# Three loads of an attention and mixer kernel made smaller: q of twelve pairs, v of all, four weight tiles

## The chip, the cores and the metric

The kernel runs on one core of a Trainium2 chip. The metric is the device time of one execution in microseconds (us). Five engines work side by side, each through its own queue in order: PE (TensorE, matmuls; PEld is its weight load), DVE (VectorE), ACT (ScalarE), POOL (GpSimd) and SP (SyncE), which here does nothing but issue transfers. The transfers themselves run on 16 DMA engines.

## The reference

Causal attention over 4 batches, 12 heads, 448 tokens and a head width of 64, and behind it two mixer blocks on the joined heads (448 tokens by 768 channels). Cut to what matters:

```python
scores = q @ k.T / 8, upper triangle masked
x = (softmax(scores) @ v), heads joined            # (4, 448, 768)

h  = relu(x.T @ w_tok1) @ w_tok2                    # tokens 448 -> 256 -> 448
u  = x + h.T
x2 = u + relu(u @ w_ch1) @ w_ch2                    # channels 768 -> 1536 -> 768

theta = x2 @ w_theta
y  = w_tok_r @ (x2 * cos(theta)) + w_tok_i @ (x2 * sin(theta))
u2 = x2 + y
out = u2 + relu(u2 @ w_ch)
```

All weights of the mixers arrive as float64 and are rounded on the chip; large products are made of fp16 pieces (high and low part, three matmuls for each product).

## The kernel before

**Pairs.** Heads are taken two at a time: 6 pairs for each of the 4 batches, 24 in all, numbered 0 to 23. Of each pair seven tiles of scores are made (`TILES`): one tile of the first 64 tokens of both heads, and for i = 1, 2, 3 one of 128 tokens for each head h. `scores` runs, for a tile, the matmuls of q and k (line 358, and 360 for the low part of k), DVE's mask and row minimum (367, tile `mx`) and ACT's exponential (369). Pairs 0 to 11 (`NATIVE`) use q and k as float32; pairs 12 to 23 are the **split pairs**, where q and k are turned into a rounded high part and a rest. For these q was put into the input twice, in partitions 0 to 63 and again in 64 to 127, and loaded whole (line 288): ACT writes the high part of all 128 partitions to `qs` (297), DVE the rest to partitions 64 to 127 (298).

**Values.** `v_raw` holds nine blocks of 64 columns for a pair. Blocks 0 to 5 are the tokens from 64 on of both heads, blocks 6 and 7 the first 64 tokens with one head each, block 8 the first 64 of both heads one above the other. Pairs 0 to 7 (`NATPV`) multiply with float32 values and transpose their attention on PE (376, copied by ACT in 378); `pv` does it on line 407. Pairs 8 to 23 split the attention into two fp16 parts (`ph`: ACT on 160, DVE on 388) and have a DMA transpose it into `pt` (line 391, on SP's queue), and multiply on lines 416 and 424. Their values are scaled and split too: `value_squares` (ACT, 124) and `value_split` (POOL writes `v_hi` on 163, DVE the rest over `v_raw` on 323).

**Units.** The channel products are 96 units, 24 for each batch, each of 18 fp16 matmuls of 448 columns (helper `mm3`, lines 231 to 233) with one weight tile `ws` of 384 KB. Each of the 24 weight tiles is first fetched raw (`raw`, 768 KB), rounded by ACT, POOL and DVE (177, 130, 185, 186), split into a `ws` tile (POOL 163, DVE 197) and stored to DRAM (`round_store`, line 581); each unit then loads its tile from there (`load_unit`, `stream_tile`, line 226). Unit n of batch 0 could load its tile only after it was stored. Tiles `ws` come from a ring of 8 buffers.

**Order.** The steps (7 tiles by 24 pairs) form one loop; `UNIT_STEPS` says at which step a unit is put in, `ROUNDINGS` at which step a weight tile is handled. Within that, a scheduler sets the order of instructions on each engine from priorities and its own estimate of durations, so an edit in one place can move work elsewhere. Names such as `w_c_1_4_115` in the orders below are weight tiles in DRAM: half 1, tile 4, and a running number (99 to 104 and 111 to 116 belong to units 12 to 23, numbers from 93 to units 24 on when they are loaded again).

Of the kernel before, what the change touches and what calls it, by code (L numbers as in the profile page):

```python
# [8 lines left out]
F32 = mybir.dt.float32  # L9
F32R = mybir.dt.float32r  # L10
F16 = mybir.dt.float16
# [7 lines left out]
P = 128  # L19
# [14 lines left out]
ROUND_BITS, ROUND_FETCH, ROUND_SPLIT, ROUND_STORE = 1, 2, 3, 5  # L34
LATE_CONVERT = 16
FIRST_UNIT, DENSE, RATE = 53, 88, (42, 29)
UNIT_STEPS = [FIRST_UNIT + n * (DENSE - FIRST_UNIT) // 14 if n < 14 else
# [17 lines left out]
def fused(ctx, tc, q, k, v, w_tok1, w_tok2, w_ch1, w_ch2, w_theta, w_tok, w_ch, out):  # L55
# [220 lines left out]
    def prep(b, pr):  # L276
        qr = ap2.tile([P, 2 * S], F32, tag="qk_raw", name="q_raw", bufs=2)
        if b * NPR + pr in NATIVE:
            kr = ap2.tile([P, 2 * S], F32, tag="kh", name="k_pad")
            for t, src in ((kr, k), (qr, q)):  # L280
                (nc.vector if b * NPR + pr == 0 else nc.gpsimd).memset(t[64:128], 0.0)
                if b * NPR + pr == 0 and t is qr:
                    for c in (slice(0, 2 * P), slice(2 * P, 2 * S)):
                        nc.scalar.dma_start(out=t[0:64, c], in_=src[b, pr, 0:64, c])
                else:
                    loads[b * NPR + pr] = nc.sync.dma_start(out=t[0:64], in_=src[b, pr, 0:64])
        else:
            loads[b * NPR + pr] = nc.sync.dma_start(out=qr, in_=q[b, pr])
            kr = ap2.tile([P, 2 * S], F32, tag="qk_raw", name="k_raw", bufs=2)
            nc.sync.dma_start(out=kr, in_=k[b, pr])  # L290
        vr = ap2.tile([P, 9 * D], F32, tag="v_raw", name="v_raw")
        nc.sync.dma_start(out=vr, in_=v[b, pr])
        if b * NPR + pr in NATIVE:
            qs, kh, kl = qr, kr, None
        else:
            qs = ap2.tile([P, 2 * S], F32R, tag="qs", name="qs")
            copy_to(pick("qhi"), qs, qr)
            rest_to(pick("qlo"), qs[64:128], qr[64:128], qs[64:128])
            kh = ap2.tile([P, 2 * S], F32R, tag="kh", name="kh")
# [14 lines left out]
    def value_split(n):  # L314
# [4 lines left out]
        power(None, scale, values.pop(n), unit)  # L319
        hi = ap2.tile([P, 9 * D], F16, tag="v_hi", name="v_hi", bufs=2)  # L320
        copy_to("P", hi, vr, scale)
# [71 lines left out]

    def twice(ap):
        return ap.unsqueeze(1).to_broadcast([P, 2, D])

    def pv(pp, i, h):
# [3 lines left out]
        if pp.native_pv:  # L401
            pt = pp.pts[i, h]
            blks = [8] if i == 0 else [6 + h] + [2 * u + h for u in range(i)]
            for u, vt in enumerate(blks):
                n = 2 * D if reg < 7 * D else D
                rhs = twice(pp.v[0][:, vt * D:(vt + 1) * D]) if i == 0 else pp.v[0][:, vt * D:vt * D + n]
                pp.pv = nc.tensor.matmul(pp.ps[:, reg:reg + n], lhsT=pt[:, u], rhs=rhs,  # L407
                                 start=(u == 0), stop=(u == len(blks) - 1))
            return
# [4 lines left out]
        if i == 0:  # L414
            for n, (blk, c) in enumerate(((0, 0), (0, 1), (1, 0))):
                pp.pv = nc.tensor.matmul(pp.ps[:, 0:2 * D], lhsT=pt[:, blk], rhs=twice(pp.v[c][:, 8 * D:9 * D]),
                                         start=n == 0, stop=n == 2)
            return
# [159 lines left out]
    def round_store(j):  # L578
        n = ROUNDINGS[j][1]
        if n >= 0:  # L580
            nc.sync.dma_start(out=jobs[n][1], in_=rounding.pop(j))
            stored.add(n)

    made = [0]
# [370 lines left out]
def _lay(inputs):  # L955
# [26 lines left out]
    zero = np.zeros_like(a0)  # L982
    for x, y in ((a0, np.where(native, a0, zero)), (np.where(native, b0, zero), b0), (a0, b0)):
        blocks.append(np.concatenate([x, y], axis=2))
# [41 lines left out]
```

## Time and profile before

| what | value |
|---|---|
| median of 3 runs | 872.34 us (870.30 to 873.48) |
| the profiled execution | 871.68 us |
| its span in the trace | 869.9 us |
| mean granted TensorE clock over the span | 0.998 |
| PE busy | 839.3 us (96%) |
| DVE, ACT, POOL busy | 598.9, 531.3, 265.6 us |
| moved by DMA | 151.99 MB, 175 GB/s on average |

The attention fills the first 500 us or so; units run beside it from about 110 us on, and the second mixer block follows. A matmul's busy time includes its way through the array, so a busy PE can still have small gaps that the rows don't show as idle.

### The profile page before, as it was taken

The numbers are of one execution on the slowest core, as the hardware profiler recorded it, in microseconds if no ns is written. First come the engines' busy times: TensorE is split into PE (matmuls) and PEld (weight loads), VectorE is DVE, ScalarE is ACT, GpSimd is POOL, SyncE is SP. The second block draws the span as 40 slices with busy tenths as digits, with TensorE's granted clock in tenths as the row PEclk, the third lists the DMA queues.
The fourth block names the chain that finished last, engine by engine and source line by source line (L and its number), as shares of the span: only waits on it lengthen the run. The fifth ranks groups of instructions, "written<-read, shape, count | busy, mean of one in ns | idle before, by whom it ended". The sixth has DMA issues, their size and how long they took to land.

```text
span 869.9 us, 16014 instructions
## 1 busy us (share of the span) xinstructions
PE 839.3 (96%) x5699; PEld 532.7 (61%) x5699; DVE 598.9 (69%) x1294; ACT 531.3 (61%) x1223; POOL 265.6 (31%) x445
## 2 busy tenths in 40 slices
PE   7999998899899999999999999999999999999997
PEld 6988856565657566576756655565555555555554
DVE  6788787999988556567774367669747548567541
ACT  6798786777767637367653276547647447456441
POOL 4366564547662220413222035331111001101000
PEclk9999999999999999999999999999999999999999
DMA  6866869999999976856475597702613123131012
GB/s 217 258 208 201 269 198 271 261 310 294 289 255 313 280 226 140 233 132 125 141 173 203 186 278 265 227 30 73 197 40 108 40 90 98 40 119 58 25 45 75
DMA packets 121024, 151.99 MB, mean 175 GB/s; under 512 B 76848, under 2 KB 88048, under 8 KB 120944
## 3 DMA queue, kind: packets, MB, share of 16 engines
q1 hardware_dynamic: 120400, 149.95, 59.4%
q0 software_dynamic: 384, 0.79, 0.4%
q8 instruction: 45, 0.74, 0.3%
q10 hardware_dynamic: 160, 0.23, 0.1%
q14 instruction: 35, 0.29, 0.1%
HBM read 110.56 MB, written 22.81 MB: 153 GB/s over the span
## 4 chain that ended last, share of the span: by engine, by line
PE 67%; DMA 10%; DVE 8%; ACT 5%; issue 5%; POOL 5%; SPq 0%; ACTq 0%; POOLq 0%; DVEq 0%
PE ps_mm L232 15%; PE ps_mm L231 15%; PE ps_mm L233 15%; DMA pt<-ph 5%; PE ps_sc L358 3%; PE ps_sc L231 3%; PE ps_sc L232 3%; PE ps_sc L233 3%; PE ps_pv L407 2%; DMA raw_w<-in_w_theta_dram 1%; PE ps_pv L424 1%; ACT junk L124 1%; ACT sb L369 1%; DVE sb L367 1%; PE ps_mm L376 1%
## 5 line engine op out<-in xcount | busy, mean ns | idle before, releaser
L231 PE MATMUL ps_mm<-h,ws 128*128 128x448 f16 x432 | 151.7, 354 | 1.6 <-DVE g L140 1.0
L232 PE MATMUL ps_mm<-h,ws 128*128 128x448 f16 x432 | 152.7, 354 | 0.1
L233 PE MATMUL ps_mm<-h,ws 128*128 128x448 f16 x432 | 152.5, 354 | 0.0
L231 PEld LDWEIGHTS <-ws 128*128 128x128 f16 x720 | 70.5, 98 | 67.2 <-issue 5.3
L233 PEld LDWEIGHTS <-ws 128*128 128x128 f16 x720 | 70.5, 98 | 63.9 <-issue 3.7
L232 PEld LDWEIGHTS <-ws 128*128 128x128 f16 x720 | 70.5, 98 | 62.5 <-issue 5.2
L369 ACT ACTIVATE sb<-sb,mx 128x320 f32<-128x320 f32 (+3 forms) x168 | 89.1, 533 | 25.6 <-DVE mx L367 25.0
L231 PE MATMUL ps_mm<-ut,ws 128*128 128x448 f16 x288 | 101.1, 353 | 1.4 <-DMA rawt<-x2d 1.3
L232 PE MATMUL ps_mm<-ut,ws 128*128 128x448 f16 x288 | 101.5, 353 | 0.8 <-DVE ut L197 0.8
L233 PE MATMUL ps_mm<-ut,ws 128*128 128x448 f16 x288 | 101.6, 353 | 0.0
L367 DVE CUSTOM_DVE_ANT_0 sb<-ps_sc,mask 128x320 f32<-128x320 f32 (+3 forms) x168 | 73.4, 455 | 17.7 <-PE ps_mm L376 11.3
L124 ACT ACTIVATE junk<-acc 128x448 bf16<-128x448 f32 x72 | 41.2, 572 | 59.1 <-DVE acc L912 41.3
L358 PE MATMUL ps_sc<-k_pad,q_raw 128*128 128x192 f32 (+3 forms) x168 | 56.9, 441 | 9.1 <-DMA k_pad<-in_k_dram 4.3
L787 POOL TENSOR_SCALAR tmp<-tmp 128x384 f32<-128x384 f32 x28 | 15.6, 556 | 148.6 <-ACT tmp L786 145.6
L388 DVE SCALAR_TENSOR_TENSOR ph<-sb,ph 128x128 f16<-128x128 f32 (+1 forms) x64 | 46.8, 736 | 19.0 <-ACT ph L160 18.3
L163 POOL TENSOR_SCALAR h<-t 128x448 f16<-128x448 f32 x48 | 35.2, 735 | 75.7 <-ACT t L497 75.2
L497 ACT ACTIVATE t<-ps_mm,c_scale 128x448 f32<-128x448 f32 x48 | 30.0, 625 | 41.3 <-PE ps_mm L233 36.2
L160 ACT ACTIVATE ph<-sb 128x128 f16<-128x128 f32 (+1 forms) x64 | 39.6, 625 | 25.6 <-DMA pt<-ph 25.3
L499 DVE TENSOR_TENSOR h<-t,h 128x448 f16<-128x448 f32 x48 | 32.0, 670 | 27.0 <-POOL h L163 26.9
L130 POOL TENSOR_SCALAR raw<-raw 128x768 f32<-128x768 f32 (+2 forms) x34 | 35.4, 1041 | 41.6 <-ACT wf L177 37.0
L231 PE MATMUL ps_sc<-th,ut 128*128 128x384 f16 x144 | 46.9, 326 | 0.0
L233 PE MATMUL ps_sc<-th,ut 128*128 128x384 f16 x144 | 46.8, 326 | 0.0
(218 smaller groups left out, 2119.4 us busy)
## 6 DMA issues: line engine op xcount, KB each, us to landing
ws<-w_c SPq DMA_DIRECT2D x120, 384.0 KB, 4.6
raw<-in_w_ch_dram SPq DMA_DIRECT2D x30, 768.0 KB, 5.6
w_c<-ws SPq DMA_DIRECT2D x30, 384.0 KB, 4.3
v_raw<-in_v_dram SPq DMA_DIRECT2D x24, 288.0 KB, 4.9
q_raw<-in_q_dram SPq DMA_DIRECT2D x12, 448.0 KB, 4.2
k_raw<-in_k_dram SPq DMA_DIRECT2D x12, 448.0 KB, 5.4
x2d<-acc SPq DMA_DIRECT2D x24, 224.0 KB, 3.8
acc<-x2d SPq DMA_DIRECT2D x24, 224.0 KB, 2.6
```

Source lines behind the costliest of these rows:

```text
L124: nc.scalar.activation(j[:, 0:src.shape[-1]], src, AF.Square, accum_out=dst)
L130: nc.gpsimd.tensor_scalar(out=dst, in0=a, scalar1=b, scalar2=c, op0=ALU.mult, op1=ALU.mult)
L160: nc.scalar.activation(dst, src, AF.Copy, scale=scale)
L163: e.tensor_scalar(out=dst, in0=src, scalar1=scale, scalar2=0.0, op0=ALU.mult, op1=ALU.add)
L231: nc.tensor.matmul(ps, lhsT=ka(a[:, 0]), rhs=kb(b[:, 0]), start=first, stop=False)
L232: nc.tensor.matmul(ps, lhsT=ka(a[:, 0]), rhs=kb(b[:, 1]), start=False, stop=False)
L233: return nc.tensor.matmul(ps, lhsT=ka(a[:, 1]), rhs=kb(b[:, 0]), start=False, stop=last)
L358: nc.tensor.matmul(ps[:, 0:n], lhsT=lhs, rhs=cut(pp.kh), start=True, stop=pp.kl is None)
L367: pp.first = nc.vector.tensor_tensor_reduce(out=sb, in0=src, in1=msk, op0=ALU.add, op1=ALU.min, scale=-0.125, scalar=3.0e38, accum_out=pp. ...
L369: pp.last = nc.scalar.activation(sb, sb, AF.Exp, bias=pp.mx[:, j:j + 1], scale=-1.0, accum_out=pp.sm[:, 2 + j:3 + j])
L388: nc.vector.scalar_tensor_tensor(out=lo, in0=both, scalar=PSC, in1=hi, op0=ALU.mult, op1=ALU.subtract)
L499: gates[0] = nc.vector.tensor_tensor(out=t[:, 1], in0=f, in1=t[:, 0], op=ALU.subtract)
```

## The change

Three things are done.

1. For the split pairs q is loaded into partitions 0 to 63 alone (224 KB in place of 448 KB). ACT makes the high part in partitions 0 to 63, and DVE writes the rest to partitions 64 to 127 from both inputs in partitions 0 to 63.
2. The block 8 of v goes away: the tile has 8 blocks (256 KB in place of 288 KB). The first 64 tokens use blocks 6 and 7 side by side. A float32 product of the second head (h = 1) then writes 64 columns where, for i = 1 and 2, it wrote 128. `v_hi` and the split have 512 columns in place of 576.
3. The weight tiles of units 20 to 23 stay in their `ws` buffer after the store and are used from there; their four loads of 384 KB go away.

```diff
+FIRST_DIRECT = 20
...
-            loads[b * NPR + pr] = nc.sync.dma_start(out=qr, in_=q[b, pr])
+            loads[b * NPR + pr] = nc.sync.dma_start(out=qr[0:64], in_=q[b, pr, 0:64])
...
-        vr = ap2.tile([P, 9 * D], F32, tag="v_raw", name="v_raw")
+        vr = ap2.tile([P, 8 * D], F32, tag="v_raw", name="v_raw")
...
-            copy_to(pick("qhi"), qs, qr)
-            rest_to(pick("qlo"), qs[64:128], qr[64:128], qs[64:128])
+            copy_to(pick("qhi"), qs[0:64], qr[0:64])
+            rest_to(pick("qlo"), qs[64:128], qr[0:64], qs[0:64])
...
-        hi = ap2.tile([P, 9 * D], F16, tag="v_hi", name="v_hi", bufs=2)
+        hi = ap2.tile([P, 8 * D], F16, tag="v_hi", name="v_hi", bufs=2)
...
-            blks = [8] if i == 0 else [6 + h] + [2 * u + h for u in range(i)]
+            blks = [6] if i == 0 else [6 + h] + [2 * u + h for u in range(i)]
             for u, vt in enumerate(blks):
-                n = 2 * D if reg < 7 * D else D
-                rhs = twice(pp.v[0][:, vt * D:(vt + 1) * D]) if i == 0 else pp.v[0][:, vt * D:vt * D + n]
+                n = 2 * D if h == 0 else D
...
-                pp.pv = nc.tensor.matmul(pp.ps[:, 0:2 * D], lhsT=pt[:, blk], rhs=twice(pp.v[c][:, 8 * D:9 * D]),
+                pp.pv = nc.tensor.matmul(pp.ps[:, 0:2 * D], lhsT=pt[:, blk], rhs=pp.v[c][:, 6 * D:8 * D],
...
-            nc.sync.dma_start(out=jobs[n][1], in_=rounding.pop(j))
+            w = rounding.pop(j)
+            nc.sync.dma_start(out=jobs[n][1], in_=w)
             stored.add(n)
+            if n >= FIRST_DIRECT:
+                loaded[n] = w
```

The scheduler's order changes with it. Line numbers of the changed kernel are one higher behind the new constant, and two or three lower behind `twice`, which is gone. On SP, where the last two weight tiles of batch 0 are stored, before:

```order
L581 DMA w_c_1_4_115<-ws 128x1536
L226 DMA ws<-w_c_1_4_115 128x1536
L391 DMA_TRANSPOSE pt<-ph 128x14x128
L391 DMA_TRANSPOSE pt<-ph 128x2x128
L173 DMA raw<-in_w_ch_dram 128x1536
L581 DMA w_c_1_5_116<-ws 128x1536
...
L226 DMA ws<-w_c_1_5_116 128x1536
L226 DMA ws<-w_c_0_0_93 128x1536
```

And in the changed kernel, from the same store on:

```order
L579 DMA w_c_1_4_115<-ws 128x1536
L293 DMA v_raw<-in_v_dram 128x512
L289 DMA q_raw<-in_q_dram 64x896
L291 DMA k_raw<-in_k_dram 128x896
L392 DMA_TRANSPOSE pt<-ph 128x6x128
L392 DMA_TRANSPOSE pt<-ph 128x10x128
L227 DMA ws<-w_c_0_0_93 128x1536
L227 DMA ws<-w_c_0_1_94 128x1536
L227 DMA ws<-w_c_0_2_95 128x1536
L579 DMA w_c_1_5_116<-ws 128x1536
```

The two loads that read back what was stored just ahead of them are gone, and the loads for units 24 to 26 (numbers 93 to 95) now stand ahead of the last store.

On PE, at the first scores of pair 12 (the `ps_sc` tiles; line 358 is the product with k's high part, 360 that with its low part; `ps_mm` with `wt2` is the token product, with `ident` a transpose), before:

```order
L358 MATMUL ps_sc_2696<-kh_2447,qs_2444 128x256
L360 MATMUL ps_sc_2696<-kl_2449,qs_2444 128x256
L358 MATMUL ps_sc_2742<-kh_2447,qs_2444 128x256
L360 MATMUL ps_sc_2742<-kl_2449,qs_2444 128x256
L358 MATMUL ps_sc_2776<-kh_2447,qs_2444 128x256
L360 MATMUL ps_sc_2776<-kl_2449,qs_2444 128x256
```

And in the changed kernel:

```order
L359 MATMUL ps_sc_2696<-kh_2447,qs_2444 128x256
L361 MATMUL ps_sc_2696<-kl_2449,qs_2444 128x256
L359 MATMUL ps_sc_2742<-kh_2447,qs_2444 128x256
L454 MATMUL ps_mm_2371<-ident2_128,x1_192 128x64
L234 MATMUL ps_mm_2361<-wt2_185,h1_2323 128x448
...
L361 MATMUL ps_sc_2742<-kl_2449,qs_2444 128x256
L232 LDWEIGHTS ws_2094
L232 MATMUL ps_mm_2388<-h2_1518,ws_2094 128x448
...
L359 MATMUL ps_sc_2776<-kh_2447,qs_2444 128x256
L361 MATMUL ps_sc_2776<-kl_2449,qs_2444 128x256
```

Three tiles of scores stood in a row; now the token products stand inside the second, and seven unit matmuls ahead of the third. Through pairs 12 to 18 the scores stand on average 18 unit matmuls further back than before, with most of the products `pv` of the same pairs near their old places; from pair 20 on the two orders agree within five.

## Rows read from the trace of the kernel before

**Rows 1.** The page: busy us (share of span) and instructions of each engine.
```profile
PE 839.3 (96%) x5699; PEld 532.7 (61%) x5699; DVE 598.9 (69%) x1294; ACT 531.3 (61%) x1223; POOL 265.6 (31%) x445
```
**Rows 2.** Busy time by stretch; the first line names the columns.
```profile
core 0: us, PE busy (x) PEld busy (x) DVE busy (x) ACT busy (x) POOL busy (x), PEclk, DMA share, GB/s
0.00:125.00 125.00, 115.97 (x793) 96.94 (x794) 99.19 (x263) 98.76 (x269) 69.36 (x111) 1.00 0.71 224
125.00:310.00 185.00, 170.96 (x1387) 113.00 (x1386) 160.20 (x360) 129.64 (x313) 91.53 (x130) 0.99 1.03 278
310.00:575.00 265.00, 263.51 (x1858) 161.38 (x1857) 162.55 (x344) 142.93 (x330) 76.95 (x142) 1.00 0.67 191
575.00:870.00 295.00, 288.81 (x1667) 161.35 (x1665) 176.98 (x329) 159.97 (x312) 27.75 (x64) 1.00 0.23 74
```
**Rows 3.** Chain of waits inside 125 to 310 us, share of it by line.
```profile
by line: DMA pt<-ph 23.6%; issue 17.4%; DMA k_raw<-in_k_dram 4.1%; DMA w_c<-ws 3.7%; DVE sb L367 3.7%; ACT sb L369 3.5%; ACT ph L160 2.9%; DVE ut L197 2.6%; DVE ph L388 2.5%; DVE wf L186 2.0%; POOL f L130 1.9%; POOL ws L163 1.8%; POOL sm L4
```
**Rows 4.** Waits of PE, 125 to 310 us: total us, times, longest.
```profile
PE ps_sc L358 <- DVE mx L367: 2.7, 4, 1.0
PE ps_pv L416 <- POOL v_hi L163: 2.1, 2, 1.6
...
PE ps_pv L424 <- DMA pt<-ph: 1.1, 2, 0.8
...
PE ps_mm L231 <- DMA ws<-w_c: 0.6, 1, 0.6
```
**Rows 5.** Waits of all engines, same stretch: ACT for the attention's transposes.
```profile
ACT ph L160 <- DMA pt<-ph: 18.6, 12, 3.4
```
**Rows 6.** DMA, same stretch: total; issues with count, KB each, us to landing.
```profile
DMA packets 52210, 51.36 MB, mean 278 GB/s; under 512 B 40336, under 2 KB 41104, under 8 KB 52188
...
ws<-w_c SPq DMA_DIRECT2D x31, 384.0 KB, 6.2
...
q_raw<-in_q_dram SPq DMA_DIRECT2D x9, 448.0 KB, 4.6
...
v_raw<-in_v_dram SPq DMA_DIRECT2D x8, 288.0 KB, 5.2
...
q_raw<-in_q_dram SPq DMA_DIRECT2D x2, 224.0 KB, 7.3
```
**Rows 7.** Timeline of SP's queue, then of PE: start us, us, instruction, idle before.
```profile
247.53 0.38 SPq L581 DMA_DIRECT2D w_c<-ws  x1
253.43 0.32 SPq L226 DMA_DIRECT2D ws<-w_c  x1
...
269.33 0.36 PE L231 MATMUL ps_mm<-h,ws 128*128 128x448 f16 x1 [0.57 <-DMA ws<-w_c]
```
**Rows 8.** Groups by form: tiles, shapes, count; busy us, mean ns; idle before.
```profile
L407 PE MATMUL ps_pv<-v_raw,pt 128*128 128x128 f32 x240 | 33.8, 278 | 0.9 <-ACT pt L378 0.8
...
L163 POOL TENSOR_SCALAR v_hi<-v_raw,sv 128x576 f16<-128x576 f32 x16 | 16.4, 1024 | 0.0
...
L323 DVE SCALAR_TENSOR_TENSOR v_raw<-v_raw,sv,v_hi 128x576 f16<-128x576 f32 x16 | 15.2, 952 | 5.2 <-POOL v_hi L163 5.2
...
L167 DVE TENSOR_TENSOR qs<-q_raw,qs 64x896 fp32r<-64x896 f32 x12 | 14.2, 1180 | 0.7 <-ACT qs L160 0.3
...
L407 PE MATMUL ps_pv<-v_raw,pt 128*128 128x64 f32 x64 | 8.1, 267 | 0.0
```
**Rows 9.** Busy time by stretch, columns as in rows 2.
```profile
125.00:225.00 100.00, 90.22 (x738) 60.75 (x737) 89.95 (x201) 72.84 (x173) 56.79 (x80) 0.98 1.07 279
225.00:325.00 100.00, 95.74 (x742) 61.58 (x741) 78.10 (x175) 59.61 (x144) 37.55 (x57) 1.00 0.98 277
150.00:175.00 25.00, 22.41 (x185) 13.29 (x184) 22.77 (x52) 18.64 (x47) 14.64 (x21) 0.93 1.06 265
```
**Rows 10.** Waits of SP's queue, 300 to 330 us: total us, times, longest.
```profile
SPq L226 <- PE ps_mm L233: 9.5, 2, 7.0
```

More of the change, by code (lines that the diff above doesn't have):

```diff
@@ L392, in scores @@
         pp.pts[i] = pt
-    def twice(ap):
-        return ap.unsqueeze(1).to_broadcast([P, 2, D])
     def pv(pp, i, h):
@@ L402, in pv @@
             pt = pp.pts[i, h]
-            blks = [8] if i == 0 else [6 + h] + [2 * u + h for u in range(i)]
+            blks = [6] if i == 0 else [6 + h] + [2 * u + h for u in range(i)]
             for u, vt in enumerate(blks):
-                n = 2 * D if reg < 7 * D else D
-                rhs = twice(pp.v[0][:, vt * D:(vt + 1) * D]) if i == 0 else pp.v[0][:, vt * D:vt * D + n]
-                pp.pv = nc.tensor.matmul(pp.ps[:, reg:reg + n], lhsT=pt[:, u], rhs=rhs,
+                n = 2 * D if h == 0 else D
+                pp.pv = nc.tensor.matmul(pp.ps[:, reg:reg + n], lhsT=pt[:, u], rhs=pp.v[0][:, vt * D:vt * D + n],
                                  start=(u == 0), stop=(u == len(blks) - 1))
@@ L982, in _lay @@
     zero = np.zeros_like(a0)
-    for x, y in ((a0, np.where(native, a0, zero)), (np.where(native, b0, zero), b0), (a0, b0)):
+    for x, y in ((a0, np.where(native, a0, zero)), (np.where(native, b0, zero), b0)):
         blocks.append(np.concatenate([x, y], axis=2))
```

## The prediction

> **What bounds the kernel now.** I read the page's busy times first: PE is busy for 839.3 of 869.9 us [rows 1], so the time is PE's work and the gaps in it, some 30.6 us. Next, the same by stretch [rows 2]. From 310 us on PE idles for 1.5 us in 265, and in the last stretch for 6.2 in 295; nothing that the change touches can be worth much there, and a transfer that shrinks there is free already, since the DMA share is 0.67 and 0.23. The first 125 us hold 9.0 us of idle PE, much of it the start, at a DMA share of 0.71. The stretch that matters is 125 to 310 us: PE idles for 185 − 170.96 = 14.0 us, and the 16 DMA engines are full (share 1.03, 278 GB/s), while DVE is busy for 160.20 us (87%). So three resources are nearly full at once, and each queue runs in order, so that a late result on one holds up what stands behind it.
>
> Which of them is late? The chain of waits of this stretch says DMA more than anything else: transposes of the attention 23.6%, loads of k 4.1%, stores of weight tiles 3.7%, together 31.4% of 185 us, or 58.1 us [rows 3]. But PE itself waits mostly for the vector engines: the first two lines of its waits are DVE and POOL, 2.7 and 2.1 us, and the two DMA lines are 1.1 and 0.6 [rows 4]. The link between the two is ACT, which stood for 18.6 us until a transpose had read `ph` and its buffer could be written again [rows 5]; everything else queued on ACT stood behind that. So the DMA's fullness reaches PE at second hand.
>
> **The change, part by part.** *Bytes in the full stretch.* Nine loads of q lose 224 KB each, eight of v 32 KB each [rows 6], and four reloads of 384 KB go: 2016 + 256 + 1536 = 3808 KB, 3.9 MB of 51.36, which is 7.6%. The rest of the saving (three loads of q, sixteen of v) lies where DMA has room, and I cost it at nothing; what hides it there is the DMA share of 0.67 or 0.71, and if that cover were gone it would be three loads in twelve more. What are the 3.9 MB worth? At the most the 14.0 us that PE idles; at the least nothing. Between the two I take the DMA's part of the chain, 58.1 us, and let it shrink with the bytes: 58.1 × 0.076 = **4.4 us**. I choose this one because in a full set of engines a transfer's time to landing is mostly the queue ahead of it.
>
> *The four reloads as waits.* SP issued the store of unit 22's tile at 247.53 and the load of the same tile only at 253.43, since it had to land first [rows 7]; every transfer behind it on SP, transposes too, stood for 5.5 us. That goes. At 269.33 PE waited 0.57 us for unit 23's tile [rows 7]; that goes too, since the tile is in its buffer from the conversion on. I take **0.6 us**; the other end is nothing, if PE then waits for what came next on DVE. In exchange each of the four tiles occupies one of the 8 `ws` buffers until its unit ends, so the loads for later units wait for units that are nearer. What is queued behind those waits on SP are transposes; the price stands among the rivals.
>
> *Narrower and shorter operations.* Pairs 0 to 7 each have five products of the second head (2 for i = 1, 3 for i = 2) that write 64 columns in place of 128. A float32 product is two records here (304 records for 152 products), so 80 records at 278 − 267 = 11 ns [rows 8], 0.9 us at most; the records overlap, so I take **0.5**, the other end being nothing. In the value split of pairs 8 to 23, 512 columns for 576 make POOL's 1024 ns 114 shorter and DVE's 952 ns 106 [rows 8]; PE waited for this POOL step only twice [rows 4], so I take 2 × 0.11 plus a little for DVE, **0.3 us**, and the ends are nothing and 16 × 0.22 = 3.5 us. The first product of a pair reads two blocks in place of one block twice, with as many columns: nothing.
>
> *q's rest across partitions.* DVE's subtraction now reads partitions 0 to 63 and writes 64 to 127. The trace shows no DVE step of that kind. Its columns are the same 896, and the step before took 1180 ns with 64 partitions [rows 8], so I take no change. A gain is excluded as far as columns go; twice the time would be 9 × 1.18 = 10.6 us more on a DVE with 24.8 us of idle time in the stretch, of which PE would feel perhaps a third. ACT's high part has half the partitions and the same columns: nothing.
>
> *The order.* The scheduler moved scores of pairs 12 to 18 back behind unit matmuls. That takes nothing off PE's work and adds nothing; it changes what covers a wait. I cost it at nothing in the forecast, because units ahead of late scores also fill gaps, and put the other case among the rivals.
>
> Sum: 4.4 + 0.6 + 0.5 + 0.3 = 5.8 us. Against the profiled execution's own 871.68 us (its span 869.9 and 1.8 around it) that is **866 us**. The median of the runs is 872.34, 0.7 us above the profiled execution; I don't add that. A difference of about 0.5%, 4.4 us, is what a measurement of this kernel can tell from no change, so below 868.0 is faster and above 876.7 slower.
>
> **The rivals.** *The q loads don't get cheaper.* Of the same stretch the two loads of q that were already 224 KB on 64 partitions landed after 7.3 us, the nine of 448 KB on 128 partitions after 4.6 [rows 6]. For it: the half load was no faster at all. Against it: two loads, issued at the stretch's start beside others, and the landing tells of the queue as much as of the load. Without q's part 1792 KB, 1.83 MB or 3.6%, remain: 58.1 × 0.036 = 2.1 us, and with the other terms 3.5 us, so **868.2 us**, just within 0.5%. Here the Trainium skill bears on the row: its page "SBUF — State Buffer", section "Door 1: The DMA port swizzle", says that the bandwidth of a transfer depends on how many of the 16 ports its partitions reach, and its table gives partitions 0 to 63 only the eight even ones, so a load that is halved in this way would run at half the rate. By that rule q's term is zero and the sum is this rival's; the two rows above agree in direction, but do not settle it.
>
> *The DMA was not what PE lacked.* PE's direct waits for DMA are 1.7 us of 14.0 [rows 4], and DVE at 87% could hold the pace by itself. Then only the small terms count, at most 1.4 us: **870.3 us**, no change. Against it stand ACT's 18.6 us [rows 5].
>
> *Slower: less cover between scores and products.* In pairs 12 to 18 the scores moved back by 18 unit matmuls on average and most of the products did not. A unit has 18 matmuls, so about one unit less lies between a pair's scores and the moment when PE needs the transposed attention; in between lie DVE, ACT, DVE again and a transpose. The place is 225 to 325 us. There PE idled for 4.3 us before, against 9.8 in 125 to 225, where the first split attention runs with fewer units to cover it [rows 9]. If the second hundred comes to idle like the first, it costs 5.5 us; SP's waits on the ring, two waits of 9.5 us in all in 300 to 330 [rows 10], would fall earlier, into the same stretch, and hold transposes. Another 1.7 us go if the clock falls a second time as in 150 to 175, where the granted mean was 0.93 (25 × 0.07) [rows 9], one of the two levels, 1.2 GHz, for part of it after PE had idled. Together 7.2 us, less the small terms of 1.4 us: **877 us**. It decides from the point where the cover of these pairs falls short of the transposes' way by more than the DMA's relief makes that way shorter.
>
> **How the numbers follow.** Forecast 0.42: the relief is real, but it reaches PE only through other queues, and my scaling may be off by half either way (860.5 to 868). The q loads not cheaper 0.20; DMA not the lack 0.14; slower 0.24, since the order did move and an in-order machine with three full resources has no slack. The predicted time is the forecast's, 866 us. The range that holds 8 in 10 must reach to the slower case: 860.5 to 877. By itself the forecast is 860.5 to 868. From the same cases: faster by over 0.5% 0.43, within 0.5% 0.34, slower 0.23.
>
> **What would show it.** The forecast is right if in 125 to 310 us the moved bytes fall to about 47.5 MB, the DMA share falls below 1, ACT's wait for transposes falls below 18.6 us, and PE's idle time falls to about 9 us, with the stretch from 310 us on unchanged but earlier. The first rival is right if a q load of a split pair still takes 4.6 us or more to land and the share stays at 1.03. The second, if ACT's waits fall and PE's don't. The slower case is right if PE's idle time in 225 to 325 us rises from 4.3 us, with waits of `pv` for `pt`, and SP's queue waits for units on line 227. DVE's rest of q above 1.18 us would show the partition shift as a cost. The prediction is wrong at its root if the second half of the span changes by more than 2 us.

## The result, and the profile of the changed kernel

The changed kernel takes 876.54 us (median; 873.52 to 882.69), the kernel before 871.62 us in the same runs: ratio 1.0058, 95% interval 1.0038 to 1.0079. It moves fewer bytes and is 4.9 us slower. The forecast, 866 us, had the wrong sign; the rival "slower: less cover between scores and products" had said 877.

The profiled execution took 876.86 us, its span is 875.1, 5.2 longer than that of before. First the page's line of busy times of the changed kernel (us, share of the span, instructions), beside [rows 1]:

```profile
PE 843.6 (96%) x5699; PEld 535.8 (61%) x5699; DVE 592.4 (68%) x1294; ACT 532.0 (61%) x1223; POOL 261.8 (30%) x445
```

PE is *busy* for 4.3 us more, with the same 5699 records, and idle for 31.5 us where it had been for 30.6. So between these two executions most of the difference is not waiting: the same matmuls took longer. The stretches, with the columns of [rows 2], say where:

```profile
125.00:310.00 185.00, 171.73 (x1371) 113.33 (x1370) 154.85 (x353) 129.97 (x311) 87.77 (x128) 0.97 0.96 256
310.00:575.00 265.00, 261.61 (x1837) 160.56 (x1836) 161.36 (x346) 141.67 (x329) 70.56 (x133) 0.99 0.66 187
...
225.00:325.00 100.00, 94.89 (x715) 61.14 (x716) 76.30 (x176) 61.85 (x145) 34.97 (x57) 0.97 0.90 246
325.00:425.00 100.00, 97.80 (x756) 62.86 (x755) 62.01 (x146) 56.79 (x141) 20.39 (x42) 0.98 0.64 161
150.00:175.00 25.00, 21.77 (x169) 12.65 (x170) 20.51 (x47) 16.03 (x38) 14.24 (x19) 0.93 0.89 230
225.00:250.00 25.00, 23.34 (x176) 15.68 (x177) 22.67 (x50) 19.67 (x44) 13.01 (x21) 0.93 0.97 283
300.00:325.00 25.00, 23.02 (x161) 13.67 (x158) 14.16 (x34) 9.49 (x18) 4.17 (x8) 0.93 0.66 166
350.00:375.00 25.00, 22.80 (x164) 13.06 (x164) 12.81 (x28) 8.37 (x15) 7.82 (x14) 0.93 0.73 187
```

In 125 to 310 us the DMA share is below 1 (0.96 for 1.03) and PE idles for 13.3 us instead of 14.0: the relief is there and in this order buys almost nothing. The column PEclk shows where PE's busy time grew: four stretches of 25 us have a granted clock of 0.93, where the kernel before had one (150 to 175, [rows 9]). Inside each, PE ran for 3.4 us at half the clock, 1.2 for 2.4 GHz. The two fine windows show one of these, and a normal stretch beside it:

```profile
304.70:308.10 3.40, 3.40 (x11) 1.56 (x11) 3.09 (x7) 3.37 (x6) 0.00 (x0) 0.50 0.57 135
...
296.00:299.00 3.00, 3.00 (x17) 1.56 (x16) 2.79 (x8) 1.96 (x6) 1.05 (x2) 1.00 0.69 209
```

Busy all the time in both, 11 matmuls in 3.4 us against 17 in 3.0. A half-clock stretch costs 3.4 / 2 = 1.7 us; three more are 5.1 us of the 5.2 between these two executions. What PE did ahead of three of them is in the timeline of the changed kernel (start, us, engine, line; in brackets the idle time just ahead and what ended it):

```profile
226.03 0.44 PE L359 MATMUL ps_sc<-kh,qs 128*128 128x256 f32 x1 [1.63 <-DVE mx L368]
...
303.01 0.20 PE L421 MATMUL ps_pv<-v_hi,pt 128*128 128x64 f16 x1 [1.98 <-DMA pt<-ph]
...
305.36 0.60 PE L234 MATMUL ps_mm<-ut,ws 128*128 128x448 f16 x1
305.75 0.58 PE L232 MATMUL ps_mm<-ut,ws 128*128 128x448 f16 x1
...
358.58 0.42 PE L359 MATMUL ps_sc<-kh,qs 128*128 128x320 f32 x1 [2.20 <-DVE mx L368]
```

Three single waits of 1.6 to 2.2 us, and the granted clock fell at 226.2, 304.7 and 359.3 us, each time within 2 us of the wait's end. (The fourth, at 164.8 us, stands behind a wait of 1.70 us, like that of the kernel before, at 163.9 us behind one of 1.55.) Unit matmuls then start 0.39 us apart (305.36, 305.75) where the 17 above take 0.18 each. The Trainium skill, "TensorE: Matmul & The Clock Gate", section "HAM oscillation — how this bites in real kernels", describes this pattern for a matmul that waits for DMA: the wait sends the clock back, and what comes behind it starts cold. The rows here agree in part: the clock fell behind waits for DVE as well, but not behind every wait of this length. In the kernel before PE waited 1.64 us for POOL, until 209.3 us ([rows 4]: longest 1.6), and 1.71 us for DVE, until 223.7 us, and the clock held behind both:

```profile
PE ps_mm L448 <- DVE g L140: 1.7, 1, 1.7
```

So a wait as long as the one at 226 us stood near that place before; those at 303 and 358 us, 4.2 us together, have no wait as long near them in the kernel before.

**The falls of the clock are little of the difference between the kernels.** The mean granted clock is on record for each execution, not only for the two profiled ones. For the kernel before it was 0.998 in the profiled one, but 0.9946 on average (0.990 to 1.000) over the 104 executions that were timed beside the experiments below; for the changed kernel 0.992 in the profiled one and 0.9939 on average (0.990 to 1.000) over its 14. Since a stretch at half clock costs half its length, the falls cost (1 - clock) x span: 4.7 us before, 5.3 changed. Of the 5.1 us between the means of these executions (871.6 and 876.7 us) the falls are 0.6, which is no more than the scatter of the 14; one execution of the changed kernel shows a clock of 1.000 and took 873.62 us all the same. The other 4.5 us were not lost to falls. No trace of these executions is kept, but PE's own work (its busy time less what half clock costs) is 834 to 838 us in each of the sixteen profiled executions of this document, so by this estimate most of the 4.5 us is waiting. A fall can also stand in for a wait: by a straight line through the 104 executions of the kernel before, 1 us more of half-clock cost goes with only 0.45 us more of time. The two profiled executions thus show what a fall looks like, and overstate what falls have to do with the loss.

Where the two profiled executions part can be read by adding up PE's own work from the start: they are level until about 287 us, the changed one falls back by some 7 us until 365 us, and behind 425 us it gets about 1 us back.

### The profile page after: what moved, and what is told of

Its sections match the earlier page's. It is cut to its first block, busy times and chain, and to the rows that moved or that the text cites. A ratio compares the mean times of both kernels' runs of the same rounds, so it can differ in the third digit from the quotient of the medians.

```text
span 875.1 us, 16033 instructions
## 1 busy us (share of the span) xinstructions
PE 843.6 (96%) x5699; PEld 535.8 (61%) x5699; DVE 592.4 (68%) x1294; ACT 532.0 (61%) x1223; POOL 261.8 (30%) x445
## 4 chain that ended last, share of the span: by engine, by line
PE 68%; DMA 10%; DVE 6%; issue 6%; POOL 5%; ACT 4%; SPq 0%; ACTq 0%; POOLq 0%; DVEq 0%
PE ps_mm L232 16%; PE ps_mm L233 15%; PE ps_mm L234 15%; DMA pt<-ph 5%; PE ps_sc L359 4%; PE ps_sc L232 3%; PE ps_sc L234 3%; PE ps_sc L233 3%; PE ps_pv L404 2%; DMA ws<-w_c 2%; DMA v_raw<-in_v_dram 1%; PE ps_mm L377 1%; POOL ws L164 1%; PE ps_pv L421 1%; DVE ph L389 1%
## 5 line engine op out<-in xcount | busy, mean ns | idle before, releaser
L233 PE MATMUL ps_mm<-ut,ws 128*128 128x448 f16 x288 | 102.5, 356 | 2.2 <-DVE ut L198 2.1
L232 PE MATMUL ps_mm<-ut,ws 128*128 128x448 f16 x288 | 102.5, 357 | 1.4 <-ACT ut L161 1.1
L234 PE MATMUL ps_mm<-ut,ws 128*128 128x448 f16 x288 | 102.7, 357 | 0.0
L389 DVE SCALAR_TENSOR_TENSOR ph<-sb,ph 128x128 f16<-128x128 f32 (+1 forms) x64 | 44.9, 708 | 24.8 <-ACT ph L161 24.6
L787 POOL TENSOR_SCALAR tmp<-tmp 128x384 f32<-128x384 f32 x28 | 15.5, 554 | 147.1 <-ACT tmp L786 144.1
L164 POOL TENSOR_SCALAR h<-t 128x448 f16<-128x448 f32 x48 | 31.6, 660 | 75.8 <-ACT t L494 75.5
L232 PE MATMUL ps_sc<-th,ut 128*128 128x384 f16 x144 | 46.9, 326 | 0.0
L234 PE MATMUL ps_sc<-th,ut 128*128 128x384 f16 x144 | 46.8, 326 | 0.0
L233 PE MATMUL ps_sc<-th,ut 128*128 128x384 f16 x144 | 46.6, 326 | 0.0
```

The source lines that it names most:

```text
L164: e.tensor_scalar(out=dst, in0=src, scalar1=scale, scalar2=0.0, op0=ALU.mult, op1=ALU.add)
L232: nc.tensor.matmul(ps, lhsT=ka(a[:, 0]), rhs=kb(b[:, 0]), start=first, stop=False)
L233: nc.tensor.matmul(ps, lhsT=ka(a[:, 0]), rhs=kb(b[:, 1]), start=False, stop=False)
L234: return nc.tensor.matmul(ps, lhsT=ka(a[:, 1]), rhs=kb(b[:, 0]), start=False, stop=last)
L389: nc.vector.scalar_tensor_tensor(out=lo, in0=both, scalar=PSC, in1=hi, op0=ALU.mult, op1=ALU.subtract)
```

## The experiments

**What is tested.** Theory "order": the edits made the scheduler choose another order, and that order costs the time; the data of the change help. Rival "data": something in the new code costs time itself (q's rest across partitions, the held weight tiles, the value tile). Both kernels have the same instructions on PE, DVE, ACT and POOL, one for one, some with fewer columns or partitions; on SP four loads are missing. So an order can be taken from one and given to the other: at the end of the program each instruction is tied to follow the one that a table puts ahead of it on its engine, without any wait added.

```diff
     run(todo, DT)
+    pin_orders(tc)
...
+        for a, b in zip(order[:-1], order[1:]):
+            tc.add_manual_dep(ins[b], ins[a].name,
+                              mybir.DependencyInfo(mybir.DependencyClass.NoSync, mybir.DependencyReason.DATA),
+                              reason="order")
```

**The control**, the kernel before tied to its own order:

> Control: the kernel before, bound instruction for instruction to the order that it has anyway. All theories: the same as the kernel before within the noise, ratio 0.998 to 1.002, 870 to 873 us. If it is slower or faster by more, binding an order has a price of its own, and the pinned runs have to be read against this one.

Measured: 870.82 us, ratio to the kernel before 0.9993 (0.9979 to 1.0008). Tying costs nothing that can be seen. All ratios below are to the kernel before, too.

**Code and order crossed.** First the changed code in the order of before:

> The changed kernel, with every engine and SP's queue bound to the order of the kernel before (the four reloads that it no longer has are left out). Theory 'order': the loss is what the scheduler's new order costs, three new waits of PE of about 2 us each with a 3.4 us stretch at half clock behind each, and the smaller transfers themselves help a little. Then this kernel is at or below the kernel before: 866 to 871 us, ratio 0.994 to 0.999, one 25-us window at a granted clock of 0.93 and not four, PE idle in 225-325 us at 4 to 5 us. Rival 'data': something in the new code itself costs time (the held weight tiles, the subtraction across partitions, the value tile of eight blocks), whatever the order: then it stays at 875 to 878 us, ratio 1.004 to 1.008. If it falls in between, both have a share, and its size is read from the ratio.

Measured: 869.28 us, ratio 0.9974 (0.9959 to 0.9988). Then the code of before in the changed order:

> The kernel before, all its bytes, with every engine bound to the order of the changed kernel (SP's queue too, but for the loads of weight tiles in the middle third, which stay where the scheduler puts them, since the four reloads need places). Theory 'order': it is as slow as the changed kernel or a little slower, 875 to 879 us, ratio 1.004 to 1.009, with new waits of PE near 226, 303 and 358 us and the granted clock at 0.93 in the windows behind them. Rival 'data': 870 to 873 us, ratio 0.998 to 1.002, one window at 0.93.

Measured: 879.77 us, ratio 1.0121 (1.0086 to 1.0156). So four corners, as ratios to the kernel before:

| | order of before | changed order |
|---|---|---|
| code of before | 0.9993 (0.9979 to 1.0008) | 1.0121 (1.0086 to 1.0156) |
| changed code | 0.9974 (0.9959 to 0.9988) | 1.0058 (1.0038 to 1.0079) |

Across, the order costs 0.8% with the new code and 1.3% with the old, 7 and 11 us (9 by the medians; one of the six runs behind the 11 took 888 us); down, the data give back 0.2 to 0.6%, 2 us in the good order and 5 to 6 in the bad one. The rival "data" falls: the new code isn't slower in either order, though in the good one its gain over the tied control lies within the intervals. One reserve stands against the old code in the changed order: its weight loads on SP in the middle third were not tied, and PE's waits for weight tiles make up 7.5 us there. So the 11 us, and the 5 to 6, hold the places of these loads too, and the clean price of the order is the 7 us of the new code. Of these, (1 - clock) x span gives the falls 1.8 us: the mean clock is 0.9959 in the order of before and 0.9939 in the changed one. The stretches 125 to 225, 225 to 325 and 325 to 425 us of the changed code in the order of before (columns as in [rows 2]):

```profile
125.00:225.00 100.00, 91.14 (x734) 61.34 (x732) 88.52 (x199) 72.13 (x172) 55.97 (x79) 0.97 1.02 267
225.00:325.00 100.00, 97.58 (x761) 63.52 (x760) 78.73 (x177) 60.45 (x147) 38.17 (x57) 1.00 0.93 247
325.00:425.00 100.00, 100.00 (x787) 65.60 (x786) 66.53 (x153) 61.63 (x156) 25.13 (x45) 1.00 0.61 156
```

and of the code of before in the changed order, with the first of PE's waits in 125 to 425 us (total us, times, longest):

```profile
125.00:225.00 100.00, 89.35 (x741) 60.42 (x739) 87.53 (x197) 71.04 (x170) 56.44 (x77) 1.00 1.05 268
225.00:325.00 100.00, 91.36 (x701) 58.73 (x702) 74.66 (x173) 61.26 (x145) 35.61 (x56) 0.98 0.97 274
325.00:425.00 100.00, 97.68 (x756) 63.25 (x754) 63.76 (x145) 56.67 (x141) 21.98 (x37) 0.98 0.64 164
```

```profile
PE ps_mm L316 <- DMA ws<-w_c: 7.5, 3, 3.4
PE ps_pv L509 <- DMA pt<-ph: 7.1, 7, 2.2
PE ps_sc L443 <- DVE mx L452: 4.3, 3, 2.3
```

PE idles for 11.3 us in these 300 us in the one and for 21.6 in the other. The granted clock falls once in the first, at 136 us and for 6.8 us, and twice in the second, at 269 and 361 us; the theory had said one stretch of 25 us at 0.93 for the first, which is about half of that. For the second it had named waits near 226, 303 and 358 us: the trace has 1.2, 1.4 and 2.3 us at 226, 307 and 361, and its longest two, 3.4 and 3.2 us at 209 and 269, are waits for weight tiles.

**The three parts alone**, the scheduler free:

> Only the third part of the change: the last four converted weight tiles go to their units without a reload; the scheduler orders as it likes (its order differs from that of before in 317 of 5439 places on PE, the changed kernel's in 1779). Theory 'order': little moved, little changed: 869 to 873 us, ratio 0.997 to 1.002, one or two windows at 0.93. Rival 'data' with the held tiles as its culprit: the wait of SP and of PE near 303 us appears here too, 873 to 877 us, ratio 1.002 to 1.006.

> Only the first part: q of split pairs loaded once, its rest subtracted across partitions; the scheduler orders as it likes (920 of 5439 places on PE differ from before). Theory 'order' names no time for an order that nobody has looked at: 868 to 877 us, and the time above 870 us should equal what the windows at a granted clock of 0.93 beyond the one of before cost (1.7 us each) plus the PE waits ahead of them. Rival 'data' with the subtraction across partitions as its culprit: the duration of line 167's subtraction rises above 1.18 us, or DVE waits longer in front of it, and the time rises by more than 2 us without new clock windows.

> Only the second part: the value tile of eight blocks and the narrower native value products; the scheduler orders as it likes (1647 of 5439 places on PE differ from before, the most of the three parts). Theory 'order': slower than before by what new waits of PE and half-clock stretches cost, 872 to 879 us, ratio 1.001 to 1.009, although PE's own work is 1.9 us shorter. Rival 'data': none of its own bytes can cost time, so 868 to 870 us, ratio 0.996 to 0.999.

Their edits are the parts of the change's diff. Measured: held weight tiles 875.33 us, ratio 1.0051 (1.0031 to 1.0071), slower than the theory had said for so small a change of order; q 878.49 us, 1.0092 (1.0071 to 1.0113), also above what was named for it; v 875.08 us, 1.0037 (1.0019 to 1.0054). The first expectation counted a time of 873 to 877 us for the rival, but the rival's own mark, a wait near 303 us, is not there: the new wait of 2.0 us is one for `mx` at 309.9 us, and the granted clock falls three times. q's rest across partitions took 1.13 us in the second, so the culprit named there is absent too. Each part alone gets its own order. That each of these orders is worse than the one it replaced follows if the parts themselves cost nothing, which the crossed runs show for all three together and, further below, for the first two; the three orders were not tied to the old code one by one.

**What is left of the time.** For each profiled run I take PE's idle time in 125 to 425 us (300 less the three busy times) and what half-clock stretches there cost (half their length in the trace's record of the granted clock), and subtract both from the span:

| run | span | idle | half clock | rest |
|---|---|---|---|---|
| before | 869.9 | 14.0 | 1.7 | 854.2 |
| before, tied to its own order | 868.9 | 15.2 | 0 | 853.7 |
| changed | 875.1 | 15.5 | 6.8 | 852.8 |
| changed, order of before | 866.7 | 11.3 | 3.4 | 852.0 |
| before, changed order | 878.0 | 21.6 | 3.4 | 853.0 |
| held tiles alone | 873.5 | 15.2 | 5.1 | 853.2 |
| q alone | 875.4 | 16.0 | 8.5 | 850.9 |
| v alone | 876.1 | 16.7 | 6.8 | 852.6 |

The spans reach over 11 us, the rest over 3; with the other profiled runs below it stays between 850.3 and 854.2. So these two, in this one third of the program, are nearly all that tells these executions apart. It is one execution of each; how the sum splits into waits and half clock changes between executions of one kernel, as the clocks above show.

**Which places.** The next run keeps the changed order up to 285 us and takes that of before from there:

> The changed kernel in its own order up to the instructions that run at about 285 us, and from there in the order of the kernel before. Theory 'order, at three places': in PE's own work the changed kernel is level with the others until 285 us and loses everything behind it, at 303 and 358 us; so this kernel should lose the two late waits and the two half-clock stretches behind them and come to 868 to 871 us, ratio 0.995 to 1.000. Rival 'the damage is done early' (the order of the first 285 us leaves DVE, the transposes or the weight tiles late, and the waits come whatever follows): 874 to 878 us.

Measured: 872.01 us, ratio 1.0003 (0.9986 to 1.0019), 1 us above what the theory allowed and 2 below the rival. Most of the loss is gone: PE is busy for 100.00 us of 325 to 425, and of the late falls of the clock one is left, at the change-over (290 us). So most of the damage isn't done ahead of 285 us. The same with the change-over at 230 us:

> As the run that changes over to the order of before at 285 us, but changing over at about 230 us. Theory 'order': the stretch from 230 us on is then that of the first pinned run, which loses nothing behind 225 us, and the first 230 us are those of the changed kernel, up to 3 us ahead of the first pinned run or level with it: 866 to 870 us, ratio 0.994 to 0.998, so the best version or as good as the best. Rival 'the join costs': a new wait at the change-over, 871 to 873 us as with the later join.

Measured: 875.29 us, ratio 1.0043 (1.0030 to 1.0055): a miss, above the rival's 871 to 873 as well. Behind the join PE waited 3.8 us for a transpose, until 239 us, and the clock fell for 6.8 us at 237. The join had a price of its own, so this run doesn't tell what the order behind 230 us is worth.

**One wait at a time.** These change the order of PE alone, in the changed kernel. First the wait at 358 us:

> The changed kernel in its own order but for two matmuls on PE: the two products of one score tile of pair 18 stand ahead of that pair's 57 value products and not behind them, as they do in the kernel before. Theory 'cover': the wait of 2.20 us at 358.58 us and the half-clock stretch of 3.4 us behind it (worth 1.7 us) both go: 876.5 - 3.9 = 872.6 us, ratio to the kernel before 1.000 to 1.004. Rival 'the clock falls anyway': only the wait goes, 874.3 us, and the fall turns up a little later. Rival 'DVE is late as a whole': the wait only moves to another tile, 876 to 877 us.

```diff
+MATMUL ps_sc_5372<-kh_4957,qs_4954 128x320
+MATMUL ps_sc_5372<-kl_4959,qs_4954 128x320
 ...
-MATMUL ps_sc_5372<-kh_4957,qs_4954 128x320
-MATMUL ps_sc_5372<-kl_4959,qs_4954 128x320
```

Measured: 875.54 us, ratio 1.0046 (1.0028 to 1.0065). The third reading was nearest, though its 876 to 877 us were a little too high; the wait came along with the scores, 6 us earlier:

```profile
352.57 0.41 PE L441 MATMUL ps_sc<-kh,qs 128*128 128x320 f32 x1 [2.10 <-DVE mx L450]
```

So moving the score tile does not remove the wait; DVE was late. DVE's timeline of the changed kernel shows it: `mx`, which frees the bank for the scores, stands behind 4 us of `ph` and `h`.

```profile
354.26 0.79 DVE L389 SCALAR_TENSOR_TENSOR ph<-sb,ph 128x640 f16<-128x640 f32 x1
...
355.74 0.97 DVE L496 TENSOR_TENSOR h<-t,h 128x448 f16<-128x448 f32 x1 [0.25 <-POOL h L164]
356.64 1.08 DVE L389 SCALAR_TENSOR_TENSOR ph<-sb,ph 128x896 f16<-128x896 f32 x1
357.64 0.61 DVE L496 TENSOR_TENSOR h<-t,h 128x448 f16<-128x448 f32 x1
358.17 0.35 DVE L368 CUSTOM_DVE_ANT_0 sb<-ps_sc,mask 128x192 f32<-128x192 f32 x1
```

Then that edit together with one at 303 us:

> As the run before, and at 303 us the 13 matmuls of two units that stand behind the value products of pair 16 are put ahead of the second batch of them, where PE waits 1.98 us for their transpose (13 matmuls of 0.19 us each are 2.5 us). Theory 'cover': another 2.0 us of waiting and 1.7 us of half clock go, so 872.6 - 3.7 = 868.9 us, ratio 0.995 to 0.999. Rival 'the clock falls anyway': 872 us. Rival 'DVE and the transposes are late as a whole': 875 to 877 us.

```diff
 MATMUL ps_sc_4447<-kh_4312,qs_4309 128x320
+MATMUL ps_mm_3900<-ut_3020,ws_3704 128x448
+... 12 more of ps_mm_3900 and ps_mm_3935
 MATMUL ps_pv_4192<-v_hi,pt 128x64
```

Measured: 873.03 us, ratio 1.0020 (1.0002 to 1.0038). And the edit at 303 us alone:

> The changed kernel in its own order but for the 13 unit matmuls put ahead of the second batch of pair 16's value products at 303 us; the score tile of pair 18 stays where the changed kernel has it. Theory 'the wait at 358 us is the aftermath of the one at 303 us' (DVE and the transposes fall behind there and have no slack until then): both waits go, as in the run with both edits, 872 to 874 us, ratio 1.001 to 1.003, PE idle in 325-425 us under 1.2 us. Rival 'it is the place of the score tile itself': the wait of about 2.2 us near 358 us stays, PE idle in 325-425 us 2 us or more, 874 to 876 us.

Measured: 872.65 us, ratio 1.0014 (0.9997 to 1.0030), so the edit at 303 us does all of it, and PE's idle time in 325 to 425 us is 1.1 us for 2.2. PE's longest wait for `mx` in 345 to 370 us, in the changed kernel, with the scores moved, and with the 303 us place alone covered:

```profile
PE ps_sc L359 <- DVE mx L368: 2.2, 1, 2.2
```

```profile
PE ps_sc L441 <- DVE mx L450: 2.1, 1, 2.1
```

```profile
PE ps_sc L441 <- DVE mx L450: 0.9, 1, 0.9
```

The wait at 358 us was for the most part the aftermath of the one at 303: covering the first took most of the second away, and the falls of the clock at 304.7 and 359.3 us were not there either. But in the same trace a fall came at 110.4 us, and that at 223 us lasted 6.8 us instead of 3.4; over the executions of the two kernels the mean clock gives the falls 1.6 us of the 3.9 us gained, hardly more than the scatter. Thirteen matmuls in another place are worth some 4 us, of the 7.3 between the two orders; the run with both edits had promised 868.9 and kept half of it.

**Does the price of the reloads depend on the place?** The changed kernel without its third part, in either order:

> The changed kernel without its third part (the four weight tiles are loaded again), every engine bound to the order of the changed kernel, SP's queue but for the weight loads in the middle third. It stands between the changed kernel (876.5 us) and the kernel before in the changed order (879.8 us). If what the changed kernel saves in this order is the wait for the four reloads (line 'ws <- w_c' made PE wait 7.5 us in the run of before in this order, 0.2 us in the changed kernel), it is 878.5 to 881 us, ratio 1.008 to 1.011, with PE waits for ws of 4 us and more in 125-325 us; if it is the bytes of q and v, 875 to 878 us, ratio 1.004 to 1.007, and waits for ws under 2 us.

> The changed kernel without its third part (the four weight tiles are loaded again), every engine and SP's queue bound to the order of the kernel before. Against the first pinned run (869.3 us, ratio 0.997) it tells what the four reloads cost where the order is good; in the changed order they cost 0.37% (880.3 against 876.5 us). If a reload costs by its bytes, wherever it stands, this run is as slow as that: 872 to 873 us, ratio 1.000 to 1.002. If it costs only where the order leaves it no time (the kernel before shows 0.6 us of waiting for such a load in 125-310 us), 869 to 870 us, ratio 0.996 to 0.999.

Measured: 880.26 us, ratio 1.0095 (1.0073 to 1.0117) in the changed order, with a wait of 3.2 us for one of these loads in 225 to 325 us, and 870.87 us, ratio 0.9989 (0.9971 to 1.0007) in the order of before, with one of 0.9. PE's waits for `ws` there, in the first and in the second:

```profile
PE ps_mm L316 <- DMA ws<-w_c: 3.2, 1, 3.2
```

```profile
PE ps_mm L318 <- DMA ws<-w_c: 0.9, 1, 0.9
```

Against 1.0058 and 0.9974 with the tiles held, the reloads cost 0.4% in the one, and in the other 0.15% that the intervals don't separate from nothing. One reserve: in the changed order SP's weight loads were left to the scheduler, so part of the 0.4% may be where it put them. The two intervals of the changed order also touch.

**A better version?** The changed code in the order of before is one. On top of it I covered the longest wait left in it:

> The changed kernel in the order of the kernel before, with 12 matmuls of a unit (2.3 us) put ahead of four transposes of the token mix at 137 us, for which PE waits 2.3 us in the first pinned run and 1.5 us in the kernel before; behind that wait the first pinned run had two half-clock stretches, 6.8 us. Theory 'cover': 1.5 to 2.3 us of waiting and up to 3.4 us of half clock go, 864 to 867 us, ratio 0.992 to 0.996. Rival 'the clock falls anyway', at 165 us as in the kernel before: 867 to 868 us. Rival: the wait turns up behind the moved matmuls, 869 us.

```diff
+MATMUL ps_mm<-ut,ws 128x448, 12 of one unit
 MATMUL ps_mm<-ident_128,x_191 128x64
 MATMUL ps_mm<-ident,x_191 128x128 x3
 ...
-MATMUL ps_mm<-ut,ws 128x448, 12 of one unit
```

Measured: 869.11 us, ratio 0.9972 (0.9956 to 0.9988), the same as without: the last rival was right. The wait at 137 us went, one of 2.0 us for a transpose came, which ended at 150.6 us, and one that ended at 224 us grew from 1.7 to 2.9, each with a fall of the clock behind it. Both versions beat the kernel before by about 0.3% and the changed one by about 0.8%.

## Why the prediction was wrong

**The step that failed is "The order ... I cost it at nothing".** It was the largest term of all: 7 us at the new code, against a sum of 5.8 us for everything else. The prediction had seen the order move, had a price for it among the rivals (7.2 us), and gave it 0.24. Its reason for nothing, that units ahead of late scores also fill gaps, is not what the runs show: with the same code PE idled for 15.5 us of 125 to 425 us in the changed order and for 11.3 in the order of before. The bytes, 4.4 us, were mis-sized besides.

**Bytes, 4.4 us.** The bytes fell as worked out, and the share with them (rows of the changed kernel in 125 to 310 us):

```profile
DMA packets 51117, 47.35 MB, mean 256 GB/s; under 512 B 40272, under 2 KB 41040, under 8 KB 51095
...
q_raw<-in_q_dram SPq DMA_DIRECT2D x10, 224.0 KB, 4.6
...
pt<-ph SPq DMA_TRANSPOSE x38, 4.7
```

The transposes landed after 4.7 us for 5.0 before, 6% for 7.6% of the bytes, so the scaling was fair for a transfer. ACT's wait for them fell only from 18.6 [rows 5] to 17.2 us, and PE's idle time from 14.0 to 13.3 us, not to 9. The false step was to take the DMA's part of the chain as time of PE: PE's waits there end on DVE, POOL and ACT as well. That a transpose which lands 0.3 us sooner just lets the next of these be last is a reading that no run tests by itself. With the order held still, all terms together gave 2.3 us (871.62 × 0.0026; 1.0 to 3.6 by the interval), or 1.7 against the tied control, not 5.8.

**Reload waits, 0.6 us.** Right in kind: SP's wait of 5.5 us [rows 7] is gone, and PE's wait for `ws` fell from 0.6 to 0.2 us. Where the order is worse they are worth more, as the two runs above show.

**Narrower products, 0.5 us.** About right in size, but not as a gain of each record. In the timeline of the changed kernel (start, us) eight records of either width stand in a row:

```profile
27.88 1.05 PE L404 MATMUL ps_pv<-v_raw,pt 128*128 128x128 f32 x8
30.49 1.00 PE L404 MATMUL ps_pv<-v_raw,pt 128*128 128x64 f32 x8
```

The narrow row is 0.05 us shorter, and so are shorter rows of the same trace (0.78 for 0.83 us with six records, 0.56 for 0.61 with four): whatever the number of records, the gain is the same. The trace has the second record of a narrow row start 0.056 us behind the first, in place of 0.112, and all later ones 0.112 us apart at either width. Sixteen rows became narrow (pairs 0 to 7, i = 1 and 2), so by estimate the term is 16 × 0.05 = 0.8 us, too little to be told apart in the time.

**Value split, 0.3 us.** The operations shrank: `v_hi` on POOL from 1024 [rows 8] to 833 ns, by more than forecast, DVE's rest from 952 to 858, by a little less. What PE got of it can't be told apart in these runs.

**q's rest across partitions, nothing.** Right: 1146 ns for 1180 [rows 8].

**The rivals.** "The q loads don't get cheaper" was half right: a load of 224 KB lands after 4.6 us, as one of 448 KB did [rows 6], while k's loads, unchanged at 448 KB, came down from 5.5 to 4.3 us; this agrees with the Trainium skill's "SBUF — State Buffer", section "Door 1: The DMA port swizzle". But the share fell by 6.8% (1.03 to 0.96) for 7.8% of the bytes, so it did not fall as if q had saved nothing. "DMA was not what PE lacked" is nearest to the data's part. "Slower: less cover" had the kind right, an order that leaves PE less cover, and met the time, 877, by luck, with other pieces: it had put 5.5 us of idle PE into 225 to 325 us and one more fall of the clock, 1.7 us. In the profiled execution there were 0.9 us there (5.1 for 4.3), 2.2 us in 325 to 425, where it had expected nothing, and three more falls, 5.1 us; over all executions the falls were 0.6 us. Its second reason, SP waiting longer for the ring of weight buffers, did not show: 9.5 us on line 227 in 225 to 330 us, 10.0 before. The sentence "from 310 us on unchanged" failed as well: PE idled for 3.4 us in 310 to 575, where it had for 1.5, and the clock fell at 359.3 us. Two bounds of the prediction don't come out of its own working: "off by half either way" gives 863.8 to 868.2 us, not 860.5 to 868, and the slower sum is 877.5.

**What stays open.** Which feature of the changed order first makes the transpose late at 303 us was not isolated, nor why the scheduler took it. Whether the falls of the clock follow from the waits is open: the run that covered one wait lost two falls in its trace, but falls also come and go by themselves. A wait of 1.6 to 1.7 us that ends near 224 us stands in most of the traces; the clock holds behind it in the kernel before, in the control and in the changed code in the order of before, and falls at it in the three runs that move matmuls at 303 or 358 us. That the rest of the loss is waiting is an estimate from the profiled executions.

## What to carry to other kernels

Where a scheduler sets the order, an edit that shrinks a transfer also draws a new order, and on a machine with three nearly full engines that draw can be worth more (here 7 us of 870) than the bytes (2 us in the same order). Compare the orders before the bytes, put the price of the moved work into the forecast and not among the rivals, and hold the good order fixed: the same change is then 0.26% faster and not 0.58% slower. A share of a chain that runs through other engines is no price for a relief: here it was taken as 4.4 us, and all terms together gave 2.3. And don't explain a difference of half a per cent by one profiled execution of each kernel: look at what the other executions say of the same quantity first.

## What the runs showed of the hardware

Four times in the profiled execution of the changed kernel a wait of PE of 1.6 to 2.2 us in the middle of dense work was followed by 3.4 us at half the granted clock, 1.2 for 2.4 GHz; in other runs such a stretch lasted 6.8 us (at 136 and at 237 us). Behind waits of 1.6 and 1.7 us in the kernel before, and behind the one of 2.0 us at 309.9 us with the held tiles alone, the clock held, so the length of one wait doesn't decide. Since PE is busy in these stretches, no view of waits shows them, only the clock column and a busy time that grew (843.6 for 839.3 us) at an equal count of records.

How many falls an execution has is in part chance: the mean clock of one and the same kernel lay between 0.990 and 1.000 over 104 executions, which is 0 to 9 us of half-clock cost, and 1 us of it went with 0.45 us of time.
